# Two MLPs behind a gated attention: the opening's loads, filler and order rearranged

## The chip, the cores and the metric

One core of a Trainium2 chip (trn2). The metric is the time of one execution on the device in microseconds (us); lower is better. The core has five engines that run side by side, each through its own list of instructions in order: PE (TensorE, matmuls), DVE (VectorE), ACT (ScalarE), POOL (GpSimd) and SP (SyncE, which here only starts DMA transfers). They wait for one another, and for the landing of transfers, on semaphores.

## The reference

A recurrence over 768 steps for 4 batches of 8 heads, and two MLPs on its output (3072 tokens of 384 features, 2048 hidden):

```python
f = 1.0 / (1.0 + np.exp(-f_logit))
for t in range(S):
    state = f[:, :, t, :, None] * state + np.einsum('bhd,bhe->bhde', k[:, :, t], v[:, :, t])
    y[:, :, t] = np.einsum('bhd,bhde->bhe', q[:, :, t], state)
...
x = relu(x @ w_in) ** 2 @ w_out
h = x @ w2_in
x = (h * np.tanh(softplus(h))) @ w2_out
```

All of it is float32. The weights reach the kernel as 8-byte numbers, and each is split on the chip into a high and a low half for the matmuls.

## The kernel before, in words

The attention is cut into 24 units (a chunk of 64 steps for half of the batches). A unit loads its gates and its k and q (672 KB, 112 partitions) and its v (two transfers of 96 KB). DVE and ACT turn the gates into running products: `v_min` clamps, `a_exp` and `a_ln` take the logarithm, `v_scan` sums along the chunk, `a_dq` and `a_dk` give the decays, `v_q` and `v_k` apply them. PE then transposes k (`m_t`) and forms the scores (`m_a`); DVE masks these (`v_mask`); `m_y` gives the outputs and `m_u` the state's update, which `v_s` carries on. `a_y`, `m_x`, `a_x` and `v_x` turn the output into columns of the MLP's input.

Four units make a block of 512 tokens. The first MLP runs over 6 blocks and 16 slices (`fc`) of the hidden layer: `do_l1 i` is nine matmuls into one PSUM bank (L346), `act_a` squares its rectified result on ACT, `act_b` forms the low part `gl` on DVE (L370), and `do_l2 i` is nine matmuls into three accumulators (L357); the second of each three reads `gl`. The second MLP comes after it and isn't touched by the change.

A slice's weights `w` are loaded as one tile `r` of 768 KB (`load_w`). `a_top` copies 16 bits of each 8-byte number into the upper half of a word, as float16 (L262); `w_f` ors the lower bits in (L266); `w_hi` rounds to the matmul's format on ACT (L287) and `w_lo` takes the rest on DVE (L292).

The order of all this up to the 17th `do_l2` is written out by hand: the string START lists operations, and a loop at the end of `attention` calls them in that order. An engine's list is the order in which its instructions come out of that loop. What START doesn't name is placed by the function `run`, the same in both kernels. All loads are issued by SP, in START's order; an issue waits for an earlier transfer that used the same one of eight semaphores, and for the readers of the buffer that it writes. `m_warm n` issues filler matmuls of 128 columns whose result is not used. Before START, POOL writes constants: the two `top` tiles, the identity `idn`, the mask, and zero rows of `kn` and `vs`.

Of the kernel before, what the change touches and what calls it, by code (L numbers as in the profile page):

```python
# [40 lines left out]
a_ln 0; load_f 0; load_f 1; v_scan 1; v_scan 0; a_dq 0; a_dk 0; load_v 0; v_min 2; v_min 3; v_q 0 0; a_exp 2;
load_f 2; v_k 0; load_v 2; a_ln 2; v_q 0 1; load_v 1; a_dq 1; v_scan 2; a_dk 1; v_k 1; v_q 1 1; m_t 0; v_end 1; m_a 0;
a_exp 3; m_warm 2; m_t 1; a_ln 3; v_q 1 0; v_mask 0 0; v_end 0; v_scan 3; m_warm 2; m_a 1; v_mask 0 1; a_kn 0;
v_mask 1 0; m_u 0; a_dq 2; a_dq 3; v_mask 1 1; v_s 0 1; a_dk 2; load_v 3; load_f 3; a_kn 1; v_k 2; m_warm 1; m_y 0;
v_q 2 1; m_y 1; v_s 0 0; a_dk 3; m_t 2; a_y 1; load_w 0; load_f 4; v_k 3; m_u 1; a_kn 2; v_q 3 1; m_t 3; a_y 0;
load_w 1; v_q 3 0; a_top 0; v_end 3; m_warm 2; m_a 3; v_s 1 1; v_q 2 0; m_a 2; v_min 4; v_s 1 0; a_kn 3; m_x 1;
v_mask 3 0; a_exp 4; m_x 0; a_ln 4; v_mask 3 1; load_w 2; v_mask 2 1; v_mask 2 0; m_y 3; w_f 0; a_x 1; a_x 0; a_top 1;
v_x 1; m_y 2; a_y 3; v_end 2; w_hi 0; load_w 3; load_w 4; v_x 0; m_x 3; a_y 2; load_w 5; w_f 1; a_top 2; m_warm 1;
m_x 2; w_lo 0; a_x 3; a_x 2; m_u 2; load_f 6; w_hi 1; v_x 3; v_x 2; w_f 2; a_top 3; w_lo 1; m_u 3; w_f 3; a_top 4;
w_hi 2; do_l1 0; w_f 4; act_a 0; w_lo 2; w_hi 3; a_top 5; load_f 5; v_s 3 0; v_min 5; load_w 14; load_w 9; act_b 0;  # L50
w_lo 3; do_l1 1; v_s 2 1; act_a 1; v_s 2 0; a_exp 5; do_l1 2; load_w 6; w_hi 4; act_b 1; v_s 3 1; w_f 5; act_a 2;
v_scan 4; w_hi 5; load_w 7; do_l2 0; a_ln 5; v_min 6; a_dq 4; a_dk 4; do_l1 3; do_l2 1; w_lo 4; act_b 2; a_top 6;
w_lo 5; v_end 4; w_f 6; do_l1 4; v_scan 5; load_w 11; act_a 3; load_v 6; do_l2 2; load_w 8; act_b 3; w_hi 6; v_k 4;
a_top 7; do_l1 5; w_f 7; load_w 10; act_a 4; a_exp 6; v_q 4 1; v_q 4 0; w_hi 7; a_dq 5; m_t 4; w_lo 6; do_l2 3;
a_top 9; act_b 4; v_q 5 1; a_dk 5; m_a 4; v_mask 4 1; v_q 5 0; a_ln 6; load_v 4; do_l2 4; act_a 5; v_mask 4 0;
load_f 7; a_top 8; v_scan 6; do_l1 6; a_dq 6; m_y 4; a_kn 4; v_k 5; act_b 5; w_f 9; w_f 8; m_a 5; m_u 4; w_lo 7;
v_mask 5 0; a_y 4; v_min 7; act_a 6; v_q 6 1; load_v 5; v_mask 5 1; m_t 5; v_s 4 0; w_hi 9; act_b 6; a_dk 6; v_k 6;
v_q 6 0; a_exp 7; w_hi 8; a_ln 7; a_kn 5; v_s 4 1; do_l1 7; v_scan 7; m_y 5; w_lo 9; a_top 10; do_l2 5; m_a 6;
load_w 15; load_w 13; m_t 6; w_lo 8; do_l2 6; w_f 10; m_x 4; v_mask 6 1; a_y 5; act_a 7; act_b 7; v_end 5; m_x 5;
a_kn 6; a_dq 7; a_top 11; load_f 8; load_v 7; a_dk 7; a_x 4; a_x 5; v_end 6; v_mask 6 0; do_l1 8; v_min 8; load_w 12;  # L60
v_q 7 1; a_exp 8; w_f 11; v_x 4; v_k 7; a_ln 8; m_u 6; m_u 5; do_l2 7; v_x 5; v_scan 8; v_s 5 0; m_y 6; act_a 8;
a_dq 8; m_t 7; v_s 5 1; act_b 8; v_q 8 1; do_l1 9; w_hi 11; v_q 8 0; v_s 6 1; a_dk 8; v_k 8; v_s 6 0; w_lo 11;
w_hi 10; a_y 6; w_lo 10; do_l2 8; a_kn 7; a_top 12; load_v 9; act_a 9; m_a 8; w_f 12; v_q 7 0; load_v 8; do_l1 10;
m_a 7; v_mask 8 1; v_end 7; v_mask 8 0; m_y 8; w_hi 12; m_t 8; load_f 9; a_top 13; act_b 9; act_a 10; act_b 10; a_y 8;
a_kn 8; do_l1 11; w_lo 12; v_mask 7 0; act_a 11; v_min 9; w_f 13; do_l2 9; load_v 10; m_x 6; a_exp 9; do_l2 10;
w_hi 13; a_top 15; a_top 14; a_ln 9; v_mask 7 1; m_y 7; a_x 6; a_y 7; w_lo 13; w_f 14; v_end 8; do_l1 12; act_b 11;
v_scan 9; a_dq 9; do_l2 11; do_l1 13; w_f 15; w_hi 14; act_a 12; m_x 7; w_hi 15; w_lo 14; v_x 6; a_x 7; act_b 12;
do_l1 14; do_l2 12; w_lo 15; act_a 13; act_b 13; act_a 14; m_u 7; v_s 7 0; v_x 7; do_l1 15; load_f 10; do_l2 13;
act_b 14; a_dk 9; v_s 7 1; do_l1 16; v_q 9 0; act_a 15; v_k 9; act_b 15; do_l2 14; v_end 9; v_q 9 1; y_dma 8;
# [888 lines left out]
```

## Time and profile before

| | |
|---|---|
| median of 3 runs | 918.82 us (917.06 to 919.91) |
| the profiled execution | 920.62 us, its span 918.9 us |
| PE busy | 898.9 us of the span |
| DVE, ACT busy | 656.4, 632.1 us |
| DMA | 89.94 MB, mean 98 GB/s over the span |

The span runs from the first to the last instruction of the profiled execution. PE's matmuls are pipelined, so that a busy PE says only that it had work.

### The profile page before, as it was taken

The page shows a single profiled execution, that of the slowest core. Times are in us where ns is not written, and L with a number is a line of the kernel's source. Part 1 is how long each engine was busy: PE and PEld are TensorE (multiplying, and loading weights), DVE is VectorE, ACT ScalarE, POOL GpSimd, SP SyncE. Part 2 cuts the span into 40 slices and gives each one's busy share as a digit, 9 for nine tenths or more (in the row PEclk, how much of TensorE's full clock was granted, in tenths as well). Part 3 has the DMA queues.
Part 4 walks back from the last instruction along what each step waited for, and adds up shares of the span by engine and source line. Part 5 has one row for each costly group of instructions (what it writes and reads, how often), then busy time and mean ns, then how long its engine had stood idle before and what let it go on. Part 6 is the DMA issues. An engine that isn't in the chain of part 4 may idle for free.

```text
span 918.9 us, 15245 instructions
## 1 busy us (share of the span) xinstructions
PE 898.9 (98%) x5893; PEld 727.8 (79%) x5893; DVE 656.4 (71%) x1114; ACT 632.1 (69%) x1147; POOL 6.6 (1%) x23
## 2 busy tenths in 40 slices
...
GB/s 230 320 237 117 84 18 69 147 180 183 179 136 219 127 198 167 194 113 73 164 194 137 69 1 1 70 0 1 69 1 0 70 1 1 70 0 1 35 1 38
DMA packets 34288, 89.94 MB, mean 98 GB/s; under 512 B 5216, under 2 KB 11360, under 8 KB 34208
## 3 DMA queue, kind: packets, MB, share of 16 engines
...
q8 instruction: 48, 0.79, 0.4%
...
## 4 chain that ended last, share of the span: by engine, by line
PE 96%; ACT 1%; issue 1%; POOL 0%; DVE 0%; ACTq 0%; POOLq 0%
PE h L346 44%; PE a L357 44%; PE y L538 2%; PE tr L499 1%; PE aq L484 1%; PE at L489 1%; PE uq L551 1%; PE y L531 1%; PE u L556 1%; PE warm L626 0%; ACT kn L521 0%; PE a L854 0%; ACT top L262 0%; PE xt L590 0%; ACT es L439 0%
## 5 line engine op out<-in xcount | busy, mean ns | idle before, releaser
L346 PE MATMUL h<-x,w 128*128 128x512 f32 x1728 | 434.3, 396 | 0.0
L357 PE MATMUL a<-gh,w 128*128 128x512 f32 x1146 | 392.7, 397 | 0.0
L346 PEld LDWEIGHTS h<-x,w 128*128 128x128 f32 x1728 | 325.3, 189 | 76.3 <-DVE w L292 0.4
L357 PEld LDWEIGHTS a<-gh,w 128*128 128x128 f32 x1146 | 215.3, 188 | 49.9
L357 PE MATMUL a<-gl,w 128*128 128x512 f32 x573 | 225.4, 394 | 0.0
L796 ACT ACTIVATE e<-e 128x512 f32<-128x512 f32 x95 | 60.1, 633 | 124.0 <-DVE e L795 124.0
L370 DVE TENSOR_TENSOR gl<-r,gh 128x512 fp32r<-128x512 f32 x96 | 66.0, 687 | 92.2 <-ACT gh L365 91.8
L357 PEld LDWEIGHTS a<-gl,w 128*128 128x128 f32 x573 | 107.8, 188 | 23.5
L795 DVE TENSOR_SCALAR e<-h 128x512 f32<-128x512 f32 x95 | 65.7, 692 | 67.2 <-PE h L346 67.0
L729 ACT ACTIVATE r<-h 128x512 f32<-128x512 f32 x96 | 56.7, 591 | 71.0 <-PE h L346 70.7
L790 ACT ACTIVATE r<-u,cst 128x512 f32<-128x512 f32 x94 | 68.0, 723 | 8.7 <-DVE u L804 2.7
L804 DVE SCALAR_TENSOR_TENSOR u<-e 128x512 f32<-128x512 f32 x95 | 65.8, 693 | 10.2 <-ACT e L796 0.7
L370 DVE TENSOR_TENSOR gl<-g,gh 128x512 fp32r<-128x512 f32 x95 | 65.7, 692 | 0.0
L792 DVE TENSOR_TENSOR e<-h,u 128x512 f32<-128x512 f32 x94 | 64.2, 683 | 0.0
L799 DVE TENSOR_TENSOR g<-e,r 128x512 f32<-128x512 f32 x94 | 64.1, 682 | 0.0
L365 ACT ACTIVATE gh<-r 128x512 fp32r<-128x512 f32 x96 | 60.7, 632 | 3.1
L730 ACT ACTIVATE r<-r 128x512 f32<-128x512 f32 x96 | 60.7, 632 | 3.1
L365 ACT ACTIVATE gh<-g 128x512 fp32r<-128x512 f32 x95 | 60.2, 633 | 2.9 <-DVE g L823 0.8
L791 ACT ACTIVATE r<-r 128x512 f32<-128x512 f32 x94 | 59.5, 633 | 3.0
L447 DVE TENSOR_TENSOR_SCAN es<-es,cap 112x520 f32<-112x520 f32 x24 | 29.6, 1235 | 8.4 <-ACT es L443 8.2
L619 DVE TENSOR_TENSOR x<-ax,x 128x384 fp32r<-128x384 f32 x16 | 8.9, 556 | 31.2 <-ACT x L615 31.2
L521 ACT ACTIVATE kn<-tr 64x192 f32<-64x192 f32 x88 | 28.3, 322 | 1.0
...
## 6 DMA issues: line engine op xcount, KB each, us to landing
r<-in_w_dram SPq DMA_DIRECT2D x16, 768.0 KB, 15.3
...
in<-in_qkf_dram SPq DMA_DIRECT2D x18, 672.0 KB, 5.8
vs<-in_vv_dram SPq DMA_DIRECT2D x48, 96.0 KB, 5.7
...
x<-x2d SPq DMA_DIRECT2D x6, 768.0 KB, 5.1
```

The lines of the kernel that those rows point to most:

```text
L346: T.matmul(out=ps, lhsT=w[:, k * 128:(k + 1) * 128], rhs=x[:, s, k], start=(i == 0), stop=(i == 8))
L357: T.matmul(out=acc[m], lhsT=w[:, m * 128:(m + 1) * 128], rhs=gx, start=(fc == 0 and i == 0), stop=(fc == FC - 1 and i == 2))
L365: A.activation(out=gh, in_=g, func=AF.Copy)
L370: V.tensor_tensor(out=gl, in0=g, in1=gh.bitcast(F32), op=ALU.subtract)
L730: A.activation(out=r, in_=r, func=AF.Square)
L790: A.activation(out=r, in_=u, func=AF.Ln, bias=two)
L791: A.activation(out=r, in_=r, func=AF.Exp, scale=-1.0)
L792: V.tensor_tensor(out=e, in0=hp, in1=u, op=ALU.mult)
L795: V.tensor_scalar(out=e2, in0=ps, scalar1=20.0, scalar2=None, op0=ALU.min)
L796: A.activation(out=e2, in_=e2, func=AF.Exp)
L799: V.tensor_tensor(out=g, in0=e, in1=r, op=ALU.mult)
L804: V.scalar_tensor_tensor(out=u2, in0=e2, scalar=2.0, in1=e2, op0=ALU.add, op1=ALU.mult)
```

## The change

START is written anew, from its beginning to `do_l2 16`. It calls the same operations, with these differences: `load_j 2` and `load_j 3` are gone, since units 2 and 3 now load all their 672 KB at once (`load_f`); `a_top` of slices 6, 7, 9, 10, 12 and 13 becomes `w_top`, the same copy on DVE; the filler grows from 28 to 42 units at the start, and is issued up to four units wide; and 17 `hold` operations are new. `hold kind i of j` copies one word on POOL from the tile of an earlier load (kind `of`, number `j`) into the tile that the load of (`kind`, `i`) is about to write (4 is a `w`, 3 a `v`, 2 and 0 a unit's gates, k and q). The copy must wait until the earlier load has landed, and the later load must wait for the copy. POOL writes the identity first, then the zero rows of `kn`, and the `top` tiles last.

```diff
-m_warm 14; load_j 1; eye_kn 1; v_min 1; load_j 0; load_j 2; eye_kn 0; a_exp 1; v_min 0; a_ln 1; load_j 3; a_exp 0;
...
+m_warm 28; eye_kn 0; load_j 0; load_j 1; v_min 0; a_exp 0; v_min 1; a_ln 0; v_scan 0; a_exp 1; a_ln 1; load_f 2;
+v_scan 1; a_dq 0; load_f 0; v_min 2; a_dk 0; v_k 0; load_f 3; a_dq 1; load_f 1; a_exp 2; v_q 0 0; a_ln 2; m_t 0;
+a_kn 0; v_q 0 1; m_warm 3; m_a 0; hold 3 0 2 2; load_v 0; m_warm 6; m_u 0; v_min 3; v_end 1; a_exp 3; load_w 1;
...
     tops = [st_p.tile([128, DM, 2], U32, tag="sr", name="top") for _ in range(2)]
-    for t in tops:
-        G.memset(t, 0)
+
+    def row(fc):
+        if fc not in raw:
+            raw[fc] = wp.tile([128, 4 * DM + 1], U32, tag=f"w_{fc}", name=f"r_{fc}", bufs=1)
+        return raw[fc]
 
     def load_w(fc):
-        t = wp.tile([128, 4 * DM + 1], U32, tag=f"w_{fc}", name=f"r_{fc}", bufs=1)
-        nc.sync.dma_start(out=t.bitcast(U16)[:, 1:8 * DM + 1], in_=w1[fc].bitcast(U16))
-        raw[fc] = t
+        nc.sync.dma_start(out=row(fc).bitcast(U16)[:, 1:8 * DM + 1], in_=w1[fc].bitcast(U16))
...
         def load_f(i):
-            load_in(i, 1 if i < 4 else 0, 3)
+            load_in(i, 1 if i < 2 else 0, 3)
+
+        def word(kind, i):
+            if kind == 4:
+                return row(i)[0:1, 1:2]
+            if kind == 3:
+                return vsv(i)[0:1, 0, 0, 0:1].bitcast(U32)
+            return (early[i - 2] if 2 <= i < 6 else inp[i % 2])[0:1, 2 if kind == 2 else 0, 0:1].bitcast(U32)
+
+        def hold(kind, i, of, j):
+            G.tensor_copy(out=word(kind, i), in_=word(of, j))
...
         def m_warm(n):
             sm = cap.rearrange("p h t -> p (h t)")
-            for _ in range(n):
-                T.matmul(out=warm[:, 0:128], lhsT=sm[:, 0:128], rhs=sm[:, 0:128])
+            for k in range(n, 0, -4):
+                c = 128 * min(k, 4)
+                T.matmul(out=warm[:, 0:c], lhsT=sm[:, 0:128], rhs=sm[:, 0:c])
...
+        for i in range(2):
+            G.memset(kns[i][32:64, 1], 0.0)
         G.memset(cmask, 1.0)
...
-                G.memset(kns[i][32:64, 1], 0.0)
...
+        for t in tops:
+            G.memset(t, 0)
         m_warm(14)
```

The loads in the order in which SP issues them, where `j` is a unit's gates alone (224 KB), `f` the rest or, for units 2 and up in the new order, all of it, `v` both transfers of a unit, and `w` a slice: before, j1 j0 j2 j3 f0 f1 v0 f2 v2 v1 v3 f3 w0 f4 w1 w2 w3 w4 w5 f6 f5 w14 w9 w6 w7 w11 v6; after, j0 j1 f2 f0 f3 f1 v0 w1 v1 v3 w0 w4 w3 v2 w2 w8 f5 w5 w6 f4 w10 w9 f7 v6 v4 w7.

**SP, the loads of the middle of the opening.** Before (`r_5` is slice 5's tile; `in0` and `in1` hold the even and odd units' data, `early2` and `early3` that of units 4 and 5; `vs` holds v):

```order
L246 DMA r_5_571<-in_w1_dram 128x3072
L420 DMA in0_148<-in_qkf_dram 112x1536
L420 DMA early3_153<-in_qkf_dram 112x1536
L246 DMA r_14_656<-in_w1_dram 128x3072
L246 DMA r_9_658<-in_w1_dram 128x3072
L246 DMA r_6_691<-in_w1_dram 128x3072
L246 DMA r_7_708<-in_w1_dram 128x3072
L246 DMA r_11_766<-in_w1_dram 128x3072
L432 DMA vs2_156<-in_vv_dram 64x384 x2
```

After, with the semaphores that each issue waits for (`DMAHW` a landing, `Pool` a hold; the first word is the line, 3 to 17 higher than before):

```order
L423 DMA early3_151<-in_qkf_dram 112x1536 [waits DMAHW4_49,Pool_49]
L250 DMA r_5_573<-in_w1_dram 128x3072 [waits DMAHW5_49,Pool_49]
L250 DMA r_6_596<-in_w1_dram 128x3072 [waits DMAHW6_49,Pool_49]
L423 DMA early2_150<-in_qkf_dram 112x1536 [waits DMAHW7_49,Pool_49]
L250 DMA r_10_603<-in_w1_dram 128x3072 [waits DMAHW0_49,Pool_49]
L250 DMA r_9_606<-in_w1_dram 128x3072 [waits DMAHW1_49,Pool_49]
L423 DMA in1_147<-in_qkf_dram 112x1536 [waits PE_49,DMAHW2_49,Activation_49,Pool_49]
L445 DMA vs2_154<-in_vv_dram 64x384 [waits DMAHW3_49,PE_49,Pool_49]
L445 DMA vs2_154<-in_vv_dram 64x384 [waits DMAHW4_49,PE_49]
L445 DMA vs0_152<-in_vv_dram 64x384 [waits DMAHW5_49]
L445 DMA vs0_152<-in_vv_dram 64x384 [waits DMAHW6_49]
L250 DMA r_7_696<-in_w1_dram 128x3072 [waits DMAHW7_49]
```

Unit 4's data (`early2`) come behind those of unit 5 and of slices 5 and 6, and slice 7 behind unit 7 and two `v`; eight of the twelve wait for a hold themselves.

**DVE, around the first `gl`.** Before:

```order
L292 TENSOR_TENSOR w_2_630<-wbit_606,w_2_630 128x2x384
L605 TENSOR_TENSOR vs1_155<-u_610,f_449 48x384
L436 TENSOR_SCALAR early3_153<-early3_153 112x512
L370 TENSOR_TENSOR gl_660<-r_644,gh_647 128x512
L292 TENSOR_TENSOR w_3_650<-wbit_627,w_3_650 128x2x384
L605 TENSOR_TENSOR vs0_154<-u_584,f_555 48x384 x2
L370 TENSOR_TENSOR gl_695<-r_674,gh_677 128x512
```

After (L449 is `v_min`, L295 `w_lo`, L373 `gl`, L269 `w_f`, L618 `v_s`):

```order
L295 TENSOR_TENSOR w_2_601<-wbit_577,w_2_601 128x2x384
L449 TENSOR_SCALAR early2_150<-early2_150 112x512
L373 TENSOR_TENSOR gl_679<-r_650,gh_653 128x512
L269 SCALAR_TENSOR_TENSOR wbit_682<-r_4_338,top_135 128x768
L618 TENSOR_TENSOR vs0_152<-u_579,f_490 48x384
L295 TENSOR_TENSOR w_3_660<-wbit_655,w_3_660 128x2x384
L295 TENSOR_TENSOR w_4_685<-wbit_682,w_4_685 128x2x384
```

Ahead of the first `gl` stood `v_min 5`; now `v_min 4` stands there.

**DVE, around `w_lo 5`, which `do_l1 5` needs.** Before:

```order
L266 SCALAR_TENSOR_TENSOR wbit_698<-r_5_571,top_136 128x768
L447 SCALAR_TENSOR_TENSOR es1_166<-es1_166,cap_164 112x520
L436 TENSOR_SCALAR in0_148<-in0_148 112x512
L292 TENSOR_TENSOR w_4_693<-wbit_642,w_4_693 128x2x384
L370 TENSOR_TENSOR gl_747<-r_700,gh_703 128x512
L292 TENSOR_TENSOR w_5_706<-wbit_698,w_5_706 128x2x384
L266 SCALAR_TENSOR_TENSOR wbit_753<-r_6_691,top_135 128x768
```

After (L261 CAST is `w_top`):

```order
L373 TENSOR_TENSOR gl_709<-r_698,gh_701 128x512
L449 TENSOR_SCALAR in1_147<-in1_147 112x512
L261 CAST top_135<-r_6_596 128x768
L261 CAST top_136<-r_7_696 128x768
L269 SCALAR_TENSOR_TENSOR wbit_744<-r_6_596,top_135 128x768
L475 TENSOR_TENSOR mv0_156<-early2_150,eq_725 48x512
L295 TENSOR_TENSOR w_5_737<-wbit_707,w_5_737 128x2x384
L269 SCALAR_TENSOR_TENSOR wbit_772<-r_7_696,top_136 128x768
L373 TENSOR_TENSOR gl_779<-r_774,gh_777 128x512
```

The casts of slices 6 and 7 now stand ahead of `w_lo 5` (the row that writes `w_5`), with `w_f 6` and one `v_q` of unit 4.

## Rows read from the trace of the kernel before

**Rows 1.** The page's busy time (share of the span) and instructions of each engine.

```profile
PE 898.9 (98%) x5893; PEld 727.8 (79%) x5893; DVE 656.4 (71%) x1114; ACT 632.1 (69%) x1147; POOL 6.6 (1%) x23
```

**Rows 2.** The chain that ended last, 30 to 62 us, and a row of the waits.

```profile
36.87 4.96 issue
...
42.62 8.50 PE h L346 x27
...
PE u L557 <- issue: 5.0, 1, 5.0
```

**Rows 3.** Timeline of PE: start, duration, instruction, count.

```profile
1.78 8.55 PE L626 MATMUL warm<-cap 112*128 112x128 f32 x56 [1.78 <-DVE cst L635]
...
27.04 0.62 PE L626 MATMUL warm<-cap 112*128 112x128 f32 x4
...
61.40 2.25 PE L346 MATMUL h<-x,w 128*128 128x512 f32 x9
```

**Rows 4.** DMA queues from 36.9 to 41.9 us, and q8 on the page.

```profile
q1 hardware_dynamic: 212, 1.16, 96.1%
...
q8 instruction: 1, 0.02, 1.7%
...
q8 instruction: 48, 0.79, 0.4%
```

**Rows 5.** Stretches: length, busy PE, PEld, DVE, ACT, POOL, PEclk, DMA share, GB/s.

```profile
5.00:62.00 57.00, 47.76 (x546) 41.15 (x546) 43.12 (x62) 43.47 (x85) 2.64 (x9) 0.85 1.01 293
...
41.82:47.03 5.21, 5.21 (x24) 4.16 (x25) 0.99 (x2) 0.23 (x1) 0.00 (x0) 0.50 1.02 396
...
47.03:110.00 62.97, 62.96 (x622) 50.54 (x621) 53.67 (x76) 58.96 (x109) 0.00 (x0) 1.00 0.54 152
...
61.40:94.00 32.60, 32.60 (x399) 26.49 (x398) 29.76 (x44) 30.51 (x59) 0.00 (x0) 1.00 0.37 110
```

**Rows 6.** SP's issues at 41.30 and 31.46, us to landing; loads issued at 82.29, 67.32.

```profile
41.30 0.47 SPq L432 DMA_DIRECT2D vs<-in_vv_dram  x1
...
vs<-in_vv_dram SPq DMA_DIRECT2D x1, 96.0 KB, 13.6
...
31.46 0.33 SPq L246 DMA_DIRECT2D r<-in_w_dram  x1
...
r<-in_w_dram SPq DMA_DIRECT2D x1, 768.0 KB, 20.3
...
in<-in_qkf_dram SPq DMA_DIRECT2D x1, 672.0 KB, 4.9
...
r<-in_w_dram SPq DMA_DIRECT2D x1, 768.0 KB, 4.5
```

**Rows 7.** Timeline of DVE: start, duration, instruction, count, idle before it.

```profile
17.16 0.68 DVE L511 TENSOR_TENSOR mv<-at,cmask 64x512 f32<-64x512 f32 x1
...
21.15 1.41 DVE L511 TENSOR_TENSOR mv<-at,cmask 64x512 f32<-64x512 f32 x2 [1.43 <-PE at L490]
...
36.30 1.02 DVE L619 TENSOR_TENSOR x<-xt,x 128x384 fp32r<-128x384 f32 x2
...
38.97 1.82 DVE L266 SCALAR_TENSOR_TENSOR wbit<-r,top 128x768 uint32<-128x768 uint32 x2
...
43.91 0.43 DVE L436 TENSOR_SCALAR early<-early 112x512 f32<-112x512 f32 x1 [0.69 <-DMA early<-in_qkf_dram]
```

**Rows 8.** DVE by line and shape: busy us, mean ns, idle before.

```profile
L266 DVE SCALAR_TENSOR_TENSOR wbit<-r,top 128x768 uint32<-128x768 uint32 x16 | 15.0, 947 | 1.9 <-ACT top L262 1.9
...
L274 DVE TENSOR_SCALAR wbit<-wbit 128x768 uint32<-128x768 uint32 x16 | 8.8, 551 | 0.0
...
L292 DVE TENSOR_TENSOR w<-wbit,w 128x768 fp32r<-128x768 f32 x16 | 15.0, 950 | 0.9 <-ACT w L287 0.8
...
L370 DVE TENSOR_TENSOR gl<-r,gh 128x512 fp32r<-128x512 f32 x96 | 66.0, 687 | 92.2 <-ACT gh L365 91.8
...
L462 DVE TENSOR_TENSOR mv<-in,eq 48x512 f32<-48x512 f32 x40 | 27.4, 685 | 0.5
```

More of the change, by code (lines that the diff above doesn't have):

```diff
@@ L39 @@
 START = """
-m_warm 14; load_j 1; eye_kn 1; v_min 1; load_j 0; load_j 2; eye_kn 0; a_exp 1; v_min 0; a_ln 1; load_j 3; a_exp 0;
[L41 to L69, printed above, removed]
@@ new lines @@
+m_warm 3; m_a 1; v_mask 0 1; m_t 1; v_scan 3; v_mask 1 1; load_w 0; hold 4 4 3 0; load_w 4; a_dq 2; v_s 0 1; m_y 0;
+a_dq 3; v_s 0 0; v_mask 1 0; v_q 2 0; v_q 2 1; m_warm 6; m_y 1; a_dk 2; hold 4 3 4 1; load_w 3; a_top 1; v_k 2;
+a_kn 1; m_warm 3; m_t 2; a_dk 3; a_y 1; hold 3 2 3 3; load_v 2; v_q 3 0; a_top 0; v_k 3; a_y 0; m_u 1; m_t 3; v_q 3 1;
+v_s 1 1; m_a 3; load_w 2; m_a 2; v_s 1 0; w_f 0; a_kn 2; v_end 3; m_x 0; v_mask 3 1; v_mask 3 0; v_end 2; a_kn 3;
+hold 4 8 3 3; load_w 8; m_x 1; m_y 3; w_hi 0; a_x 0; a_x 1; hold 2 5 4 4; load_f 5; v_mask 2 0; v_mask 2 1; m_y 2;
@@ new lines @@
+a_top 2; a_y 3; v_x 0; w_f 1; a_y 2; m_warm 1; m_x 3; a_x 3; v_x 1; w_lo 0; m_x 2; v_x 3; a_x 2; w_hi 1; a_top 3;
+hold 4 5 3 2; load_w 5; v_x 2; w_f 2; m_u 2; hold 4 6 3 2; load_w 6; hold 2 4 4 8; load_f 4; w_hi 2; hold 4 10 2 5;
+load_w 10; hold 4 9 4 5; load_w 9; m_u 3; do_l1 0; w_lo 1; hold 2 7 4 6; load_f 7; do_l1 1; a_top 4; act_a 0; w_f 3;
+hold 3 6 2 4; load_v 6; w_hi 3; load_v 4; v_s 3 1; v_s 2 0; w_lo 2; v_min 4; do_l1 2; a_top 5; act_b 0; a_exp 4;
+w_f 4; v_s 2 1; w_hi 4; act_a 1; w_lo 3; w_lo 4; a_ln 4; v_min 5; load_w 7; act_a 2; v_s 3 0; act_b 1; v_scan 4;
```

23 lines of the change are left out of this document (21 added, 2 removed).

## Prediction

> **What bounds the kernel now.** The page comes first: TensorE (PE) is busy for 98% of the span, VectorE (DVE) and ScalarE (ACT) for about 70%, GpSimd (POOL) for 1% [rows 1]. So the program is one long line of matmuls, and only what lengthens that line costs time: a gap in it, matmuls at the lower clock, or filler (the `warm` matmuls, whose result nobody reads). The chain that ended last shows where these are. From the first `do_l1` at 42.6 on it is matmuls without a break; before that it holds one large piece with no work in it, 4.96 us of "issue" from 36.87 [rows 2]. The timeline of PE gives the frame: filler from 1.78 for 8.55, the sixth layer-one group (`do_l1 5`) at 61.40 [rows 3]. I use 61.40 as a milepost: behind it the matmuls are the same in both kernels, and PE does not stand up to 110 (62.96 of 62.97 busy) [rows 5].
>
> What is the 4.96? It lies in the middle of `m_u 3`, ahead of a matmul L557 that waited for nothing [rows 2]. In that stretch the transfers of PE's own program (queue q8) appear, one of them, while the data queue holds the 16 DMA engines at 96% [rows 4]. Over the kernel q8 makes 48 transfers for 5893 matmuls and as many weight loads, some 246 instructions each [rows 1, 4]. So PE ran out of program: the next piece was asked for behind the bulk loads. The clock then pays a second time: it is at half (0.50, that is 1.2 GHz) from 41.82 to 47.03, where PE is busy throughout [rows 5], and 5.2 us at half speed is 2.6 us lost. The stall and its clock cost 7.6 us together.
>
> The third thing to see is the loads. Between 5 and 62 us the DMA engines are busy all the time, at 293 GB/s [rows 5]. The `v6` load, issued at 41.30, needs 13.6 us and lands at 54.9; `w7`, issued at 31.46, needs 20.3 and lands at 51.8 [rows 6]. Loads of 112 partitions are dear: with little beside them a 672 KB `in` takes 4.9 us to land and a 768 KB `r` 4.5 [rows 6].
>
> **The change, part by part.** *The opening up to `do_l1 0`.* 28 filler units of 128 columns become 42. The 28 took 8.55; two units at full clock take 0.62 with their tail [rows 3], so 14 more at 0.2 to 0.3 cost 3 to 4, and PE reaches `m_t 0` near 13.7. The wider form saves program, not time: 28 units were 56 matmuls and 56 weight loads [rows 3], now 11 calls make 44, so every boundary in PE's program moves 68 instructions later. `m_t 0`, 3 units and `m_a 0` then end near 16, at full clock. From there DVE sets the pace: from the first `v_mask` to the last `v_x` it has the same 29 instructions in both kernels, which took from 17.16 to 37.3 with a wait of 1.4 in it [rows 7], so 18.7. 16 + 18.7 puts the last `v_x`, and so `do_l1 0`, near 35, not 42.6. That is 7.5 sooner, and 2.6 more if the clock stays up: 10.
>
> *The holds.* 17 one-word copies on an engine that is 99% idle, at the 0.29 of its mean instruction [rows 1], cost nothing themselves. What they do is to make a load wait for the landing of an earlier one, and SP issues in order, so all behind it wait too. Counting landings at 1.9 to 2.9 us a big load, three or more big loads stay outstanding at any time, so the engines should not run dry; and the order of transfer is the order of issue with or without holds.
>
> *The loads' new deadlines.* Here the gain is lost again. Count what must land through `w7` in the new order: seven units of `f` and `j` (672 KB each), six `v` (192), eleven `w` (768): 14,304 KB. The old order through `v6` is seven, five and eleven: 14,112 KB, landed at 54.9 [rows 6]. The mix is the same, so `w7` lands at 55.0 to 55.5 in the new kernel, perhaps 1 earlier since four loads of short rows are gone. I take 55.0. Through `f4` it is six units, four `v`, eight `w`, 10,944 KB; the old order has 10,080 at `f5`, which DVE waited for until 43.91 [rows 7]. Two `w` more and one `f` less make it 43 to 46; I take 44.5.
>
> Now the order on DVE. `v_min 4` (it needs `f4`) stands ahead of the first `gl`, which the first layer-two group needs. PE has done three `do_l1` by 35 + 6.3 = 41.3; `gl` is there at 44.5 + 0.43 + 0.69 = 45.6. From `v_min 4` to the second cast (`w_top 7`, needs `w7`) DVE has 14 instructions, 10.4 by their mean durations and 9.3 if each starts 0.08 before the last one's end, as the pair at 38.97 does (1.82 for two of 0.95) [rows 7, 8]. So DVE comes to the cast at 53.8 to 54.9 and `w7` at 55.0: it starts at 55. Behind it in line are `w_f 6`, `v_q 4 1` and `w_lo 5`, and `do_l1 5` needs the last: the cast, 0.95, 0.69 and 0.95 [rows 8], less the overlap.
>
> *The cast* does not stand in the trace on DVE. From below: the one-source shift of 768 columns, 0.55; from above: the two-source pass of the same width, 0.95 [rows 8]. I take 0.95, because the shift reads whole words that lie side by side and the cast picks 16 bits out of every eight bytes. `do_l1 5` then starts at 55 + 3.2 = 58.2 (57.8 with 0.55). The Trainium skill (VectorE: DVE Perf Modes, "What auto-detection actually checks") says that an operation with one source, and both sides in SBUF, uses two ports; by that the cast is the 0.55 one. No row here shows it.
>
> *From there on* PE's work up to `do_l1 11` (six `do_l1`, five `do_l2`, attention pieces) is about that of the old stretch 61.40 to 94.0, some 33 us. DVE has 44 instructions in that stretch, three casts among them: 31.6 with the overlap, 35.1 without. It paces PE or nearly; I allow 0.8. In the old kernel ACT did the casts, and the same stretch had DVE busy for 29.76 of 32.6 [rows 5]. The clock probably falls during the wait before `do_l2 0` (3 to 4 us; in the old kernel it was down after 5), but what runs slowly then runs in the 2 us that PE would wait for `w_lo 5` anyway; 0.2 more.
>
> *Sum:* 61.4 - 58.2 = 3.2 gained, less 0.8 and 0.2: **2.2**. The profiled execution took 920.62 (span 918.9), 1.8 above the median of 918.82. Against the median: **916.6**.
>
> **The rivals.**
> *The opening's gain is kept* (0.20). For it: PE's 10 us are real, and if the loads were quicker, DVE would be at the cast at 50. Against: 293 GB/s over 57 us, at full share. `do_l1 5` at 35 + 17 = 52, the clock up: 918.8 - 10 + 1 = 909.8, or 913 if the program fetch still costs 3 us. By the Trainium skill (DMA: Bandwidth & Descriptors, "Queues, rings and completion order") a DMA engine serves a packet of typically 9 to 17 descriptors of one queue before it turns to another. A `w` is 128 rows over 16 engines, 8 each, so two waiting loads are enough for a full packet, and the holds leave three: the fetch would wait as before. 68 instructions after the middle of `m_u 3` (32 of it, 18 for each `do_l1`) the boundary meets the third `do_l1`, behind which PE must wait for `gl` anyway; so the forecast bears it.
> *DVE becomes the bound* (0.15): the other side. Six casts at 0.95 are 5.7 us more on DVE where it already was busy for 91%. If it loses the 2.8 that it stood in the old stretch and its three casts (2.8) besides, PE slips by 5.6 to 6 instead of 0.8: 918.8 - 3.2 + 6 = 921.6 and up to 924. It is slower than before from a slip of 3.2 on, measurably from 6.
> *Nothing comes of it* (0.10): both waits of PE last over 3 us, the clock falls in the second one, and 2.6 goes: 918 to 920.
>
> **How the numbers follow.** The likeliest (0.55) is gating by the loads: 914.5 to 918.5. About 0.3%, 2.8 us, can be told from no change: faster means under 916.0, slower over 921.6. Of the 0.55, 0.21 lies under 916.0 (`w7` a little sooner, the cast at 0.55); with the 0.20, faster is 0.41. The rest of it and the 0.10 make 0.44. Slower is 0.15. The range leaves out half of the kept gain below and most of DVE's case above: 910.5 to 921.5.
>
> **What the profile would show.** Right: no "issue" piece inside `m_u 3`; `do_l1 0` near 35 at full clock; DVE idle before L449 (releaser the `early` load) near 44 and before L261 (releaser `r`) near 54; PE idle before `do_l2 0` and before `do_l1 5`, which starts near 58; DMA share still 1.0 to 60. Wrong: `do_l1 5` at 52 to 54 with no DVE wait for loads (the holds made the loads quicker), or PE waiting for L295 and L373 again and again after 60 (DVE is the bound), or DMA share under 0.9 in the opening (the holds starve the queue, and everything behind comes later).

## The result, and the profile after

The changed kernel takes **924.70 us** (median of 17 runs, 920.05 to 929.60) against 918.82 for the kernel before (17 runs, 915.67 to 920.48): ratio 1.007, 95% interval 1.0052 to 1.0088. It is 5.9 us slower; the forecast was 916.6, with 921.5 as the upper end. The profiled execution took 925.11 us, its span is 923.4.

The page, the line of [rows 1]:

```profile
PE 903.4 (98%) x5859; PEld 722.2 (78%) x5859; DVE 660.3 (72%) x1120; ACT 627.9 (68%) x1141; POOL 13.7 (1%) x40
```

The timeline of PE, as [rows 3] (start, duration, instruction, idle before it):

```profile
1.77 12.46 PE L640 MATMUL warm<-cap 112*128 112x512 f32 x22 [1.77 <-DVE cst L649]
...
37.25 6.55 PE L349 MATMUL h<-x,w 128*128 128x512 f32 x27
43.64 0.40 PE L360 MATMUL a<-gh,w 128*128 128x512 f32 x1
46.65 0.50 PE L360 MATMUL a<-gl,w 128*128 128x512 f32 x1 [2.61 <-DVE gl L373]
...
57.55 0.63 PE L349 MATMUL h<-x,w 128*128 128x512 f32 x2
61.99 2.69 PE L349 MATMUL h<-x,w 128*128 128x512 f32 x7 [3.81 <-DVE w L295]
```

`do_l1 0` starts at 37.25 and not at 42.6, with no "issue" piece ahead of it. Then PE stands twice, and the lead is gone: `do_l1 5` issues two matmuls at 57.55 and its third at 61.99. In the kernel before the third came 0.46 behind the first, at 61.86, so PE is now 0.13 behind.

The timeline of DVE says for what:

```profile
45.57 0.43 DVE L449 TENSOR_SCALAR early<-early 112x512 f32<-112x512 f32 x1 [4.06 <-DMA early<-in_qkf_dram]
...
53.94 0.42 DVE L449 TENSOR_SCALAR in<-in 112x512 f32<-112x512 f32 x1
54.28 0.62 DVE L261 CAST top<-r 128x768 f16<-128x768 bf16 x1
59.03 0.60 DVE L261 CAST top<-r 128x768 f16<-128x768 bf16 x1 [4.14 <-DMA r<-in_w_dram]
...
60.99 0.94 DVE L295 TENSOR_TENSOR w<-wbit,w 128x768 fp32r<-128x768 f32 x1
```

The waits are the two that were forecast: `v_min 4` for `f4`, the cast of slice 7 for `w7`. The first ends about 1 us later than expected (45.57 for 44.5), the second 4 us later (59.03 for 55). `w7` was issued at 49.97 and landed at 58.94. Stretches of the same trace (columns as in [rows 5]):

```profile
5.00:62.00 57.00, 48.58 (x522) 34.38 (x520) 42.82 (x62) 42.28 (x82) 9.84 (x25) 1.00 1.02 271
...
62.82:66.23 3.41, 3.41 (x10) 2.67 (x9) 3.37 (x5) 3.33 (x6) 0.00 (x0) 0.50 0.18 52
61.99:94.00 32.01, 32.01 (x302) 25.79 (x303) 30.51 (x42) 26.22 (x54) 0.00 (x0) 0.95 0.31 105
```

The queue was as full as before (share 1.02), but moved 271 GB/s and not 293. Behind the second wait PE works 3.41 us at half clock, 1.7 lost. At `do_l1 19`, the first group that START does not name, PE is 2.0 late. Before, then after:

```profile
140.47 2.25 PE L346 MATMUL h<-x,w 128*128 128x512 f32 x9
```

```profile
142.43 2.27 PE L349 MATMUL h<-x,w 128*128 128x512 f32 x9
```

From there the program is the same in both kernels, yet PE loses 2.5 more. Two of its waits show it, the first matmuls of the attention's scores in two later units:

```profile
244.45 0.69 PE L497 MATMUL aq<-mv,in 48*64 48x64 f32 x32 [1.43 <-issue]
...
404.05 1.09 PE L497 MATMUL aq<-mv,in 48*64 48x64 f32 x32 [2.10 <-issue]
```

The same two before:

```profile
241.60 0.69 PE L484 MATMUL aq<-mv,in 48*64 48x64 f32 x32 [0.48 <-PE h L346]
...
400.31 0.69 PE L484 MATMUL aq<-mv,in 48*64 48x64 f32 x32 [1.12 <-issue]
```

Behind the second the clock is now at half for 3.41 us, 1.7 lost. With the two longer waits that is 3.6; elsewhere behind START the changed kernel wins 1.1 back, which was not followed up.

### The profile page after: what moved, and what is told of

Its sections match the earlier page's. It is cut to its first block, busy times and chain, and to the rows that moved or that the text cites. A ratio compares the mean times of both kernels' runs of the same rounds, so it can differ in the third digit from the quotient of the medians.

```text
span 923.4 us, 15224 instructions
## 1 busy us (share of the span) xinstructions
PE 903.4 (98%) x5859; PEld 722.2 (78%) x5859; DVE 660.3 (72%) x1120; ACT 627.9 (68%) x1141; POOL 13.7 (1%) x40
## 4 chain that ended last, share of the span: by engine, by line
PE 92%; DMA 5%; SPq 1%; issue 1%; POOL 0%; DVE 0%; ACT 0%; DVEq 0%; POOLq 0%
PE a L360 43%; PE h L349 42%; DMA early<-in_qkf_dram 2%; DMA r<-in_w_dram 2%; PE y L551 2%; PE aq L497 1%; PE tr L512 1%; DMA vs<-in_vv_dram 1%; PE uq L564 1%; PE at L502 1%; SPq L445 0%; PE y L544 0%; PE u L569 0%; PE a L871 0%; SPq L250 0%
## 5 line engine op out<-in xcount | busy, mean ns | idle before, releaser
L813 ACT ACTIVATE e<-e 128x512 f32<-128x512 f32 x95 | 60.1, 633 | 124.2 <-DVE e L812 124.2
L373 DVE TENSOR_TENSOR gl<-r,gh 128x512 fp32r<-128x512 f32 x96 | 65.9, 687 | 90.1 <-ACT gh L368 89.7
L812 DVE TENSOR_SCALAR e<-h 128x512 f32<-128x512 f32 x95 | 65.7, 692 | 67.2 <-PE h L349 66.9
L373 DVE TENSOR_TENSOR gl<-g,gh 128x512 fp32r<-128x512 f32 x95 | 65.7, 692 | 0.2 <-ACT gh L368 0.2
```

What stands on the lines that cost most here:

```text
L373: V.tensor_tensor(out=gl, in0=g, in1=gh.bitcast(F32), op=ALU.subtract)
L812: V.tensor_scalar(out=e2, in0=ps, scalar1=20.0, scalar2=None, op0=ALU.min)
L813: A.activation(out=e2, in_=e2, func=AF.Exp)
```

## The experiments

Two questions: why did `w7` come late, and where do the late losses come from? The table is the key to all runs: the median and its ratio to the kernel before on the same chip (918.73 to 919.25 there), the start of `do_l1 19` in the profile, and the span less that start, so what came behind START. For the kernel before these are 140.47 and 778.4. The profile is one execution, and executions differ by some 3 us either way; a row's profile explains its median only to that.

| run | median us | ratio, 95% interval | `do_l1 19` | behind it |
|---|---|---|---|---|
| changed kernel | 924.70 | 1.0070, 1.0052 to 1.0088 | 142.43 | 781.0 |
| e1 no holds | 926.35 | 1.0084, 1.0052 to 1.0116 | 143.58 | 782.0 |
| e2 128 rows | 914.27 | 0.9958, 0.9940 to 0.9976 | 135.19 | 781.0 |
| e3 waits later | 923.55 | 1.0054, 1.0033 to 1.0075 | 139.85 | 783.1 |
| e4 before, wide filler | 918.75 | 1.0002, 0.9981 to 1.0023 | 133.41 | 782.3 |
| e5 128 rows, shift | 914.03 | 0.9945, 0.9926 to 0.9964 | 134.78 | 777.7 |
| e6 before, 128 rows | 914.86 | 0.9958, 0.9945 to 0.9971 | 133.21 | 777.8 |
| e7 e5, cast later | 914.55 | 0.9954, 0.9936 to 0.9972 | 134.83 | 778.7 |
| e8 casts on ACT | 925.29 | 1.0063, 1.0045 to 1.0081 | 143.03 | 782.0 |
| e9 all waits later | 918.92 | 1.0004, 0.9989 to 1.0019 | 134.43 | 781.2 |
| e10 shift | 922.21 | 1.0040, 1.0022 to 1.0058 | 142.81 | 777.7 |
| e11 e2, cast later | 913.33 | 0.9954, 0.9938 to 0.9969 | 132.59 | 780.3 |
| e12 e9, 128 rows | 915.30 | 0.9970, 0.9953 to 0.9987 | 133.21 | 781.6 |
| e13 pairs | 926.59 | 1.0078, 1.0056 to 1.0100 | 140.32 | 781.1 |
| e14 e9, pairs | 917.49 | 0.9994, 0.9975 to 1.0013 | 133.62 | 781.2 |

**e1, no holds.** All 17 `hold` operations are struck from START, as here:

```diff
-hold 3 1 2 0; load_v 1; v_scan 2; load_v 3;
+load_v 1; v_scan 2; load_v 3;
```

> The changed kernel without its 17 hold operations; the order of the loads stays. Theory A (the 112-row loads slow the queue, not the holds): between 5 and 62 us the DMA engines carry 271 GB/s as they do with the holds, within 10; slice 7 lands at 57 to 60 as with them (58.9), DVE waits before its second cast for 3 to 4 us as with them (4.1), and the time is within 2 us of the changed kernel's 924.7. Rival B (the holds keep too few loads under way): the rate comes back to 290 or more, slice 7 lands at 55 or before, the second wait of DVE falls under 1, and the time falls by 4 or more, to 920 or less. A side effect under both: more loads under way, so PE's program may be fetched later, and a stall as in the kernel before may return in the opening.

Theory A. Rate and wait stay (the stretch, and the wait of the second cast):

```profile
5.00:62.00 57.00, 48.80 (x521) 35.18 (x519) 41.71 (x60) 41.45 (x82) 2.95 (x8) 0.97 1.02 269
...
60.20 0.60 DVE L260 CAST top<-r 128x768 f16<-128x768 bf16 x1 [3.71 <-DMA r<-in_w_dram]
```

The holds neither slow the queue nor cost time that can be told. Without them unit 4 landed at 46.3 (45.6 with them) and slice 7 at 60.1, just outside the forecast, and PE's first wait was longer (4.63, with the clock at half behind it); the median is 1.7 higher, which is within the intervals.

**e2, loads of 128 rows.**

```diff
-        inp = [at1.tile([112, 3, 512], F32, name=f"in{i}") for i in range(2)]
+        inp = [at1.tile([128, 3, 512], F32, name=f"in{i}") for i in range(2)]
...
-    qkf = np.zeros((NC, 2, 112, 3, H * C), a.dtype)
+    qkf = np.zeros((NC, 2, 128, 3, H * C), a.dtype)
```

> The changed kernel with the gates, k and q of a unit padded with zeros from 112 to 128 rows, so that a unit's load has 128 rows of 6 KB (768 KB for 672 KB) like a slice's; nothing else changes. Theory A (a load of 112 rows is what makes the queue slow: 6 KB packets take about 0.43 us while one is under way and 0.235 while only slices are): the packets take 0.235 to 0.26 throughout, the stretch from 5 to 55 us carries 350 GB/s or more (it carried 278), unit 4 lands near 40 in place of 45.6 and slice 7 near 49 in place of 58.9; both waits of DVE are gone or under 1 us, the sixth layer-one group starts at 53 to 56 in place of 62.0, the clock does not fall at 62.8, and the time is 914 to 918. Rival B (the holds): the packets stay slow, since what is under way is as little as before, and the time stays within 2 us of 924.7. Rival C (a 112-row load is slow because of its place in HBM, not its rows): the packets of units stay near 0.43 though slices are at 0.235, and the 14% more bytes make the time 924 to 927.

Theory A. From 30 to 35 us one unit load is under way beside slices in both kernels. The changed kernel there, then e2:

```profile
30.00:35.00 5.00, 3.68 (x74) 3.29 (x75) 4.91 (x8) 3.89 (x9) 0.80 (x1) 1.00 1.01 215
```

```profile
30.00:35.00 5.00, 4.83 (x128) 4.36 (x130) 4.86 (x9) 4.11 (x11) 1.34 (x3) 1.00 1.01 413
```

14% more bytes for a unit, and the queue moves nearly twice as much at the same share of busy engines. (The padding also moves every unit's place in HBM; no run changes the one without the other.) The first wait is gone. The second was forecast to go and did not: `w7` landed at 51.7, not 49, and PE still waits 2.03, with 3.41 us at half clock behind it:

```profile
54.75 1.43 PE L349 MATMUL h<-x,w 128*128 128x512 f32 x5 [2.03 <-DVE w L295]
```

**e13, unit loads in pairs.** `load_f 4` moved directly behind `load_f 5` (without its hold), `load_f 6` behind `load_f 7`; 112 rows.

```diff
-hold 2 5 4 4; load_f 5;
+hold 2 5 4 4; load_f 5; load_f 4;
...
-hold 2 4 4 8; load_f 4; w_hi 2;
+w_hi 2;
...
-hold 2 7 4 6; load_f 7;
+hold 2 7 4 6; load_f 7; load_f 6;
```

> The changed kernel (112 rows) with its unit loads issued in pairs: unit 4's directly behind unit 5's (its hold on slice 8 left out), unit 6's directly behind unit 7's. Bytes, rows and everything else stay. The set of loads that ends with slice 7 and unit 6 is the same in both; in the changed kernel it is complete at 62.9 us. Theory S (a 112-row load slows all that runs beside it, so two that run side by side slow the queue for little longer than one): the set is complete by 59, 4 us sooner, since the slow stretches of units 5 and 4, and of 7 and 6, lie over one another; unit 4 lands by 41 (45.6 before), so the wait of PE ahead of the first layer-two group goes. Rival T (each packet of a 112-row load takes its time whatever runs beside it): the set is complete at 62 to 63.5 as before. Under both, slice 7 itself lands with unit 6 beside it, at 59 to 63, and PE still waits for it ahead of the sixth group: 921 to 925 by S, 923 to 927 by T.

Theory S. Slice 7 and unit 6 are both in at 56.2, not 62.9; unit 4 at 38.0, not 45.6; the last load of this stretch at 59.6, not 65.7. Same bytes, same rows: two slow loads side by side cost the queue little more than one. From 30 to 35 us, where the changed kernel moved 215 GB/s, and the cast of slice 7:

```profile
30.00:35.00 5.00, 4.25 (x102) 3.80 (x104) 4.78 (x9) 3.99 (x11) 0.00 (x0) 1.00 1.00 238
...
56.32 0.60 DVE L261 CAST top<-r 128x768 f16<-128x768 bf16 x1 [6.29 <-DMA r<-in_w_dram]
```

Slice 7 is sooner than either theory had it. The time is not theory S's: 926.59 lies in T's range, and only the profiled execution (923.23, 3.4 below the median) in S's; what decides for S are the landings. The first wait is gone and PE is 2.1 us ahead of the changed kernel at `do_l1 19`, but the median is not lower: DVE was sooner at the cast, and PE waited 5.93 there, with the clock at half for 6.83 during and behind it.

**e3 and e9, the waiting instructions moved back.** e3 puts `v_min 4` behind `w_lo 4` and the cast of slice 7 behind `w_lo 5`. e9 moves also `v_min 7`, the cast of slice 6, and `w_f 7` and `w_hi 7` behind `w_lo 6`. No load moves.

```diff
-w_f 5; act_b 2; v_min 7; do_l2 0; w_top 6; a_dq 4; do_l1 3; w_hi 5; hold 3 5 4 9; load_v 5; a_dk 4; w_top 7; w_f 6;
+w_f 5; act_b 2; do_l2 0; a_dq 4; do_l1 3; w_hi 5; hold 3 5 4 9; load_v 5; a_dk 4;
...
-w_lo 6; m_t 4; a_exp 7; w_f 8; w_top 9; act_b 4; w_f 9; m_a 4; v_min 6; do_l1 6; v_end 5; a_kn 4; a_top 11;
+w_lo 6; v_min 7; w_top 7; w_f 7; m_t 4; a_exp 7; w_hi 7; w_f 8; w_top 9; act_b 4; w_f 9; m_a 4; v_min 6; do_l1 6; v_end 5; a_kn 4; a_top 11;
```

> The changed kernel with two instructions moved within the order of their engine, and no load moved: v_min 4 (with its a_exp 4 on ACT) stands behind w_lo 4 in place of ahead of the first gl, and the cast of slice 7 behind w_lo 5 in place of ahead of w_f 6. Theory A (PE lost 2.6 and 3.8 us because DVE stood in line for two loads, with 1.7 of half clock behind it): both waits of PE shrink under 1 us though the loads land when they did (45.6 and 58.9), the sixth layer-one group starts at 56 to 58, the clock stays up there, and the time falls by 5 to 8, to 917 to 920. Rival D (DVE's work with the casts paces PE anyway): PE waits for DVE a little later instead, for w_lo or gl between 58 and 100, and the time falls by under 2.5. Theory A says nothing on the 3.4 us that were lost behind 200 us; if they belong to chance, they may be gone too, and the time is 914 to 917.

> e3 carried through: of the changed kernel's four DVE instructions that wait for a late load, each now stands behind what PE needs sooner. v_min 4 behind w_lo 4; the cast of slice 6 behind do_l1 4; v_min 7, the cast of slice 7 and w_f 7 behind w_lo 6, and w_hi 7 on ACT after them. No load moves and nothing else. In e3 the wait of PE had only changed its cause (v_min 7 waited 5.5 us for unit 7, and PE 4.9 behind it). Theory A: with 112-row loads landing as before (unit 7 at 55, slice 7 at 59) PE has no wait over 1 us up to the sixth layer-one group, which starts at 52 to 54.5 (62.0 in the changed kernel), and one of at most 2 us behind it; PE is 5 to 8 us ahead of the changed kernel at 135 us, and the time is 916 to 920, the late losses staying. Rival D (DVE's work paces PE): it is under 3 us ahead at 135 us, with several waits of PE for w_lo and gl between 53 and 75, and the time is over 921.

e3 was half a miss: the first wait of PE went (0.74 is left one group later), but `v_min 7`, next in DVE's line, waited in the cast's place:

```profile
55.32 0.43 DVE L449 TENSOR_SCALAR in<-in 112x512 f32<-112x512 f32 x1 [5.48 <-DMA in<-in_qkf_dram]
```

PE then waited 4.86. e9 carried it through: `do_l1 5` starts at 53.69, and from `do_l1 0` on PE has no wait over 0.3 us up to 236.

```profile
53.69 2.26 PE L349 MATMUL h<-x,w 128*128 128x512 f32 x9
```

It is 8.0 us ahead of the changed kernel at `do_l1 19`, with the same loads, and 5.8 below it in the median. So nearly all that the late loads cost by `do_l1 19` was paid through DVE's order (e12, the same order with 128 rows, is 9.2 ahead there), and DVE's work with six casts does not pace PE. In the median e12 is 3.6 below e9, more than the 1.2 at `do_l1 19`; where the rest is won is not shown.

**e8, the casts on ACT.** Every `w_top` becomes `a_top` at its place.

```diff
-a_dk 4; w_top 7; w_f 6;
+a_dk 4; a_top 7; w_f 6;
```

> The changed kernel with its six casts back on ACT, at the same places of the order. Theory A (what the casts cost is the wait for slice 7, not their work): the wait for slice 7 is now ACT's, which has the eviction of the fourth and fifth layer-one group behind it; w_lo 5 on DVE no longer stands behind it, so the sixth layer-one group starts 1 to 4 us sooner, and PE waits for gl instead, ahead of the fourth layer-two group; in sum within 2 us of 924.7. Behind 66 us nothing changes, since there PE didn't wait for DVE. Rival D (DVE's six casts of 0.61, 3.7 us, pace PE between 62 and 130): the time falls by 3 or more, to under 921.7. Rival G (ACT is the busier one): it rises by 2 or more.

925.29: theory A. `do_l1 5` starts at 57.69 without a wait, and PE waits 3.17 ahead of `do_l2 3` instead. Where the casts run makes no difference here that can be told.

**e4, wide filler alone.** The kernel before with the new `m_warm` and nothing else.

```diff
-            for _ in range(n):
-                T.matmul(out=warm[:, 0:128], lhsT=sm[:, 0:128], rhs=sm[:, 0:128])
+            for k in range(n, 0, -4):
+                c = 128 * min(k, 4)
+                T.matmul(out=warm[:, 0:c], lhsT=sm[:, 0:128], rhs=sm[:, 0:c])
```

> The kernel before with one part of the change alone: its filler of the same 28 units is issued up to four units wide, so that PE's list is shorter by some 70 instructions ahead of the first layer-one group; order, loads and casts are those of before. Theory A (the stall of 4.96 us was PE's program arriving late, and where it strikes is set by the count of instructions): the stall leaves m_u 3; the first layer-one group starts at 36 to 39 in place of 42.6, at full clock, and the next piece of program is needed inside the layer-one groups. There PE then waits for the first gl, behind v_min 5, whose load lands at about 43.9 as before, and the sixth layer-one group starts at 57 to 60 in place of 61.4: 915 to 918. Rival E (the stall belongs to that matmul or to a resource that is not counted in instructions): it stays ahead of the same matmul, 4 to 5 us, and the time is 918 to 920. Rival F: the stall moves into the layer-one groups, where nothing hides it, and the time is 917 to 920 with an issue piece of 2 to 5 us behind 38.

The trace is as theory A has it, and the time (918.75) is not: the stall is gone, `do_l1 0` starts at 37.31, `do_l1 5` at 54.16 (sooner than forecast), PE is 7.1 us ahead at `do_l1 19` and the median is that of the kernel before. 3.9 us of it are given back behind START, in the profile, in the same two waits as in the changed kernel (1.61 and 2.34, the clock at half behind the second).

**e6, 128 rows in the kernel before.** e2's edit.

> The kernel before with one thing changed that the change doesn't touch: units' loads of 128 rows in place of 112. Theory A: the queue carries 340 GB/s or more up to 55 us (it carried 300), the loads land 5 to 8 us sooner at the end of the opening, and since a fetch of PE's program stands behind shorter bulk, the stall in m_u 3 shrinks from 4.96 to under 2 and the clock with it; the sixth layer-one group starts at 55 to 57 in place of 61.4. Fetches far behind stay where they are against y_dma, so that little is given back: 911 to 915. Rival B (PE's program is late for another reason): the stall stays at 4 to 5, nothing else waits for loads in this kernel, and the time is 917 to 919.

Theory A; a stall of 1.81 is left, in the same place:

```profile
37.07 0.24 PE L557 MATMUL u<-vs,kn 128*48 128x48 f32 x1 [1.81 <-issue]
```

The pair e4 and e6 tells most on what lies behind START: both are 7.1 to 7.3 us ahead at `do_l1 19`, and e6's median is 4.0 below the kernel before, e4's is not below it (914.86 and 918.75). In e6 the count of instructions on PE's list is that of the kernel before; in e4 it is 92 less (46 matmuls, and as many weight loads). The pair differs in the rows too. And e6, the old order with padding alone, is as low as e2, the new order with padding.

**e5 and e10, the count of instructions.** 72 more instructions of filler ahead of everything else, the same columns: in e5 with 128 rows, in e10 in the changed kernel.

```diff
-m_warm 28; eye_kn 0; load_j 0; load_j 1; v_min 0;
+m_warm 1; m_warm 1; m_warm 1; m_warm 1; m_warm 1; m_warm 1; m_warm 1; m_warm 1; m_warm 1; m_warm 1; m_warm 1; m_warm 1; m_warm 1; m_warm 1; m_warm 1; m_warm 1; m_warm 1; m_warm 1; m_warm 1; m_warm 1; m_warm 1; m_warm 1; m_warm 1; m_warm 1; m_warm 4; eye_kn 0; load_j 0; load_j 1; v_min 0;
```

> The kernel with 128-row loads (e2), and its first 28 units of filler issued as 24 single ones and one of four: the same columns in 18 more calls, 72 more instructions on PE's list ahead of everything else. The work, the order and the loads don't change; what moves is the place at which PE's program crosses from one 16 KB piece to the next. Theory P (two of the late losses, the waits of PE ahead of aq near 237 and 397 us of 1.06 and 2.35, and the clock's half level behind the second, come from a piece of program that is fetched while y_dma's small transfers run: those that lay beside a fetch landed in 3.0 to 3.7 us in place of 1.8 to 2.1): with 72 more instructions the fetches at 215 and 375 us come some 7 us earlier, outside those transfers; the landings fall to 2.2 or less, the waits to under 0.6 and 1.2, the clock stays up at 397, and the time falls by 2 to 4 against e2's 914.3, to 910.5 to 912.5. In the opening a piece is asked for near 27.8 and needed near 34.8; with the lag of 4.7 that e2 showed it comes in time. Rival Q (the waits ahead of aq are DVE's own pace): they stay at 1.06 and 2.35, and the time stays within 1.5 of 914.3. Rival R: the piece for the opening is late again, a stall of 1 to 4 us returns before 36, and the time is 914 to 918.

> The changed kernel (112 rows) with 72 more instructions of filler on PE's list, as in e5, and nothing else. In the opening it can only lose: a piece of program is needed near 30 and near 36.8, asked for 6 to 7 us before, and may come 1 to 3 us late; most of that hides in the wait for unit 4, so PE is 0 to 1.5 us behind the changed kernel at 135 us. Theory P: the fetches that lay in y_dma's transfers at 222 and 382 us are gone, PE's waits near 244 and 404 shrink from 1.43 and 2.10 to 0.3 to 0.6 and to 1.2 or less, and the clock stays up behind the second: 2 to 3.5 us are won there, and the time is 921 to 924. Rival Q (those waits have nothing to do with where the program is cut): they stay, and the time is 924.5 to 927.

e10 is the test on the changed kernel: theory P. With it PE's list is within four instructions of the kernel before, and the opening's stall is back:

```profile
39.96 0.31 PE L569 MATMUL u<-vs,kn 112*48 112x48 f32 x1 [3.43 <-issue]
```

In the order of start this is the 944th matmul or weight load of PE in the trace. The stalls before (4.96), in e6 (1.81) and in e5 (1.34) stand ahead of the 944th too, in `m_u 3`. The waits behind it take most of it up: the first is gone, and the second is 1.89 for 3.81. PE is 0.4 later at `do_l1 19` and 2.9 sooner at the end; the median falls by 2.5 (the intervals of the two ratios just overlap). SP's issues near 223 us (start, duration with the wait for a free semaphore) show where it starts, the changed kernel first:

```profile
223.26 1.53 SPq L596 DMA_DIRECT2D ax<-ay  x1
224.83 1.06 SPq L304 DMA_DIRECT2D sr<-in_w_dram  x2
```

```profile
q8 instruction: 1, 0.02, 2.1%
...
ax<-ay SPq DMA_DIRECT2D x2, 8.0 KB, 3.3
```

and e10:

```profile
223.65 0.60 SPq L596 DMA_DIRECT2D ax<-ay  x1
224.29 1.06 SPq L304 DMA_DIRECT2D sr<-in_w_dram  x2
```

```profile
ax<-ay SPq DMA_DIRECT2D x2, 8.0 KB, 1.8
```

A 16 KB piece of PE's program (q8) is fetched at 223.04 in the midst of `y_dma`'s six small transfers; those beside it land in 3.3 us, not 1.8. SP, which waits for them, issues the weights of the second MLP 0.9 later, counted from the first of the six; ACT and DVE take these later, and PE waits for DVE (L479, which writes the `in` that the scores read, ends at 244.35, and they start at 244.45). In e10 no piece is fetched there. At the six transfers ahead of the second wait one still is, against the expectation: it delays the fourth to sixth, whereas in the changed kernel it delays the sixth alone, and that one lands 0.9 later, counted from the first. PE's waits in e10 are 0.44 and 1.25, with the clock up:

```profile
243.84 0.69 PE L497 MATMUL aq<-mv,in 48*64 48x64 f32 x32 [0.44 <-PE h L349]
...
402.58 0.69 PE L497 MATMUL aq<-mv,in 48*64 48x64 f32 x32 [1.25 <-issue]
```

The second wait follows these landings over all 16 traces: the last of the six lands 4.9 to 6.8 us after the first is issued, and PE's wait, 24 to 25 us behind that issue, rises with it from 0.61 to 2.40 (e6 4.93 and 0.61, e10 5.51 and 1.25, the changed kernel 6.36 and 2.10, e11 6.82 and 2.39). The table's profiles agree: those with the old count or within four of it (the kernel before, e5, e6, e7, e10) have 777.7 to 778.7 behind START, the eleven others 780.3 to 783.1. The medians bear it out for the 112-row kernels (e10 against the changed kernel) and not for those with 128 rows (e5 against e2, e7 against e11). In e5 half of the expectation failed: the profile has the waits at 0.55 and 0.69 and is 3.7 shorter than e2's, but the medians agree (914.03 and 914.27), since e2's profile is its slowest execution; and rival R's stalls came (1.68 and 1.34). Whether the clock falls behind the second wait differs from run to run: it did after 2.10 in the changed kernel, and not after 2.39 in e11.

**e7, e11, e12, e14, combinations.** e7 and e11 move the cast of slice 7 behind `w_lo 5` in e5 and e2; e12 is e9's order with 128 rows; e14 is e9's order with e13's loads. The move in e7 and e11:

```diff
-a_dk 4; w_top 7; w_f 6;
+a_dk 4; w_f 6;
...
-do_l1 4; w_f 7;
+do_l1 4; w_top 7; w_f 7;
```

> e5 with the cast of slice 7 moved on DVE from ahead of w_f 6 to ahead of w_f 7, behind w_lo 5. In e2 that cast was the last wait for a load (3.0 us on DVE, 2.03 on PE, and 3.4 us at half clock behind it, 1.7 lost). Theory A: PE's wait before the sixth layer-one group is gone, the group starts at 51.5 to 52.5 (52.1 with the wait of 2.0 behind its second matmul in e2), the clock stays up at 56, and the time is 3 to 4 below e5: 907 to 909 if e5 comes out as theory P has it. Rival D (DVE's work with the casts is what paces PE there): PE waits for DVE a little later, and the time is within 1.5 of e5.

> e2 (128 rows, no shift) with the cast of slice 7 moved behind w_lo 5 on DVE, as in e7. In e7 it could show nothing, since PE came to that place 3.4 us later than in e2, after slice 7 had landed. Theory A: the 2.03 us that PE waited in e2 before the sixth layer-one group and the 1.7 us of half clock behind it are gone; PE is 3 to 4 us ahead of e2 at 135 us, and the time is 910.5 to 912. Rival D (DVE paces PE): PE waits within 10 us behind that place for DVE, is under 1.5 ahead at 135, and the time is within 1.5 of 914.3.

> e9's order with 128-row loads. Theory A: with the loads early and no wait in line, PE stands dense from the first layer-one group (35 to 36) on, as in e11 and no more: the same time as e11 within 1.5, 910 to 912. Rival D: moving the cast and w_f 7 further back makes DVE late with w_lo 7 or v_k 4, PE waits 1 us or more between 55 and 75, and the time is 1.5 or more above e11.

> e13's loads with e9's order on DVE and ACT. By theory S the loads come soon enough for that order and it keeps e9's lead (8 us ahead of the changed kernel at 135 us): 917 to 920. By T slice 7 comes at 60 to 63, a few us behind its place, and PE waits 1 to 3 us for it or for what stands behind it: 919 to 922.

e7 could show nothing: with the shift a piece of program was late in the opening (a stall of 1.40; 1.68 and 1.34 in e5), PE came 3.5 later than in e2 and no longer found the cast waiting. e11 removed the wait (2.6 ahead of e2) but is only 0.9 lower in the median, above the forecast. e12 is 2.0 above e11, also above its forecast, though no wait over 0.3 shows up to `do_l1 7`. In the profiles 0.6 of it is lost by `do_l1 19` and 1.3 behind, where the clock was at half for 3.41 us in e12 and not in e11; why, and whether this holds for the medians, stays open. e14 keeps e9's lead without a wait for slice 7, as theory S has it; that it is 1.4 below e9 is within their intervals. The lowest ratios are those of e5, e7, e11, e2 and e6, all with 128 rows and 0.4 to 0.6% below the kernel before, and they don't differ by more than their intervals.

## Why the prediction was wrong, point by point

- **The stall was PE's program, and its place goes by the count of instructions: right.** e4 removes it with the filler alone, and with the old count it is back at the same place (e10, e5).
- **`do_l1 0` near 35 at full clock: 37.25.** The clock was right. DVE's 29 instructions from the first `v_mask` to the last `v_x` took 20.4 (16.47 to 36.88), not 18.7.
- **The holds cost nothing: right** (e1).
- **`f4` at 44.5: 45.55, and DVE at the second cast at 53.8 to 54.9: 54.9.** The first 1.1 late but within its 43 to 46, the second right.
- **"The mix is the same, so `w7` lands at 55.0": this step failed; 58.94.** I took bytes by kind as additive. A unit's 112-row load slows everything under way beside it (215 against 413 GB/s with 128 rows), so what counts is how long such a load is under way, not how many there are. From `f5` on the new order sends them one at a time; e13 pairs them, `w7` lands at 56.2 and the same bytes are in 6 us sooner. The old order had one such pair, `f6` and `f5`, which landed at 41.2 and 43.9; that it was faster for this reason alone is not shown. The Trainium skill (DMA: Bandwidth & Descriptors, "The descriptor swizzle") says that in a transfer to 128 partitions each DMA engine writes one port of SBUF; 112 rows over 16 engines would be 7 each (an estimate from that section's 16 engines), which does not fit that split. e2's 413 against 215 GB/s do not contradict it, but no run here looks at ports.
- **The clock, 0.2: mis-sized, 1.7.** It did not fall in the first wait of PE but in the second, behind which no later wait covers the slow work. The rival that nothing comes of the change had this right.
- **The cast, 0.95: measured 0.61.** The rule of the Trainium skill (VectorE: DVE Perf Modes, "What auto-detection actually checks"), by which it would be the 0.55 one, was the better guess; the trace agrees with its side, and the 0.34 between the two is small beside the 4 us by which `w7` was late.
- **DVE slips by 0.8: about 0.1** (what is left of the 2.0 at `do_l1 19` after 0.13 and 1.7), though DVE was busy for 30.51 of 32.01. The rival that DVE becomes the bound came nearest to the measured time (921.6 to 924), by luck: its mechanism did not take place (e8, e9).
- **"Behind the milepost the matmuls are the same in both kernels": true, and the second step that failed.** The same matmuls were cut into pieces of program 68 instructions away, and the fetches fell on `y_dma`. The term was put at nothing, and it was 2.5 in the profile; e10 gives it back.

In sum, against 2.2 gained: 0.1 lost at the milepost, 1.7 by the clock, 0.1 that may be DVE's, 2.5 behind START, 4.5 between the two profiled executions. The medians differ by 1.4 more; the profiled execution before was 1.8 above its median, that of after 0.4.
